# Attention scores in two 288-key halves, and the transposed q and k of a head pair side by side in one tile

## Chip, core and metric

One core of a Trainium2 chip runs the whole program. The metric is the time of one execution on the device, in microseconds (us); the time of a kernel is the median of its runs. The engines are TensorE (PE; its weight loads are shown as PEld), VectorE (DVE), ScalarE (ACT), GpSimd (POOL) and SyncE (SP). SP computes nothing here: it issues most of the transfers, in the order of its queue. Each engine works through its own queue in order.

## What is computed

Attention with a position bias, and two mixture-like feed-forward blocks behind it. The attention part is what the change touches.

```
B, H, S, D = 4, 8, 576, 64
scores = q @ k.T / sqrt(D) + bias[h]        # bias: a small network on log distances, per head
attn   = softmax(scores)
x      = attn @ v                            # 2304 tokens x 512
h      = max(x @ w1, x @ w2, x @ w3) @ w_out
out    = (sigmoid(h @ g) * (h @ u)) @ w_out2
```

## The kernel before

**Precision.** A float32 matrix is held as two float16 parts, high and low. Products are sums of float16 matmuls over such parts.

**Units and pairs.** There are 32 heads of 576 rows; a head has five row tiles (four of 128 rows, one of 64). Two heads make a pair P, and the ten units of a pair are its row tiles, the two heads in turn. The main loop runs over u, the 160 units. In iteration u it emits, among others: `emit_E` of unit u, `emit_X` (the exp), `emit_S` of unit u + 1, the later stages of units before, pieces of the first MoE (`moe1`, matmuls of 288 columns in `mm3`, line 797) as filling for TensorE, and at the end `prep(u)`. For the first eight heads (`by_pe`) TensorE transposes the attention weights itself (line 690) and GpSimd scales them (line 659); for the others SP transposes them by DMA (`emit_T`, line 702), and of every ten units some are worked on by GpSimd (lines 659 and 674).

**`prep`, the preparation of q and k.** It runs some 16 units ahead, by steps s of a pair (s = u + 16 - 10 P):
- steps 0 and 1: `load_qk`, q and k of both heads from HBM by SP (lines 359 and 360);
- steps 2 to 6: squares and scales;
- steps 6 and 7: `r_hi` for q, then for k, on GpSimd (line 402), steps 8 and 9: `r_lo` on VectorE (line 407). They write tile `R`, both heads at once;
- steps 10 and 11: `r_trans` (line 411), one DMA transpose on SP each, 1280 columns. Before, the one at step 10 is for the first head of the pair, q and k mixed, and that at step 11 for the second head;
- steps 14 and 15: `k_swap` for the first and the second head (lines 421 and 422): two VectorE copies that exchange the upper and lower 64 partitions of k (high and low part), into tile `k2`.

For pair 0 the transposes are at steps 8 and 9 and the swaps at 11 and 12, ahead of the main loop.

**`emit_S`** (lines 617 and 618) multiplies the q tile of a unit with k and then with k2, four matmuls: 512 columns into the first PSUM bank of a score tile and 64 into the second, twice. There are two score tiles. `put_sums` puts one-column matmuls (line 130) behind them into free columns of the same tile. **`emit_E`** (line 637) is one VectorE operation: scores plus bias, and the maximum of each row.

`v_shift` (lines 452 and 453) makes similar copies of v, at iterations 7 and 8 of ten, `v_hi` (line 440) its high part on GpSimd.

Of the kernel before, what the change touches and what calls it, by code (L numbers as in the profile page):

```python
# [11 lines left out]
F16 = mybir.dt.float16  # L12
# [3 lines left out]
ALU = mybir.AluOpType  # L16
# [48 lines left out]
def tile_kernel(ctx, tc, q, k, v, w1, b1, w2, mw1, mw2, mw3, mwo, gw, vw, ow, xtab, masks, out):  # L65
    nc = tc.nc
    B, H, S, D = q.shape
# [4 lines left out]
    NIT = 5  # L72
    rows = [128, 128, 128, 128, 64]
    HS = S // 2
# [34 lines left out]
    def end_tiny():  # L109
        tiny(len(tq))  # L110
# [13 lines left out]
    def put_sums(free, lag=False):  # L124

        c = 0
        now = sums[:ripe[0]] if lag else sums[:]
        for src, then in now:
            for i in range(src.shape[1]):
                nc.tensor.matmul(free[:, c:c + 1], lhsT=ones, rhs=src.bitcast(BF16)[:, 2 * i + 1:2 * i + 2],  # L130
                                 start=(i == 0), stop=(i == src.shape[1] - 1))
            summed.append((then, free[:, c:c + 1]))
            c += 1
        del sums[:len(now)]
        ripe[0] = len(sums)
# [25 lines left out]
    with tc.manual_schedule():  # L161
# [31 lines left out]
        def rpool(name, bufs):  # L193
            return at.enter_context(tc.tile_pool(name=name, bufs=bufs, side="right"))

        p1, p2, p3, p4 = rpool("p1", 1), rpool("p2", 2), rpool("p3", 3), rpool("p4", 4)
# [145 lines left out]
        kq_t, k2_t, v_t = {}, {}, {}  # L342
# [4 lines left out]
        R_t, qs_t, vs_t = {}, {}, {}  # L347
        rqk2 = slots[3][:, 0:1280].rearrange("p (j h t d) -> p j h t d", j=2, h=2, t=NIT)

        def rq(P):  # L350
            return rqk2 if P in (2, 4) else rqk
# [45 lines left out]
        def r_hi(P, j):  # L397

            if j == 0:
                R_t[P] = p1.tile([128, 2, NIT, 2, 2, D], F16, tag="R", name="R")  # L400
            s = qs_t[P][:, j:j + 1]
            nc.gpsimd.tensor_scalar(R_t[P][:, :, :, j, 0], rq(P)[:, j], s, 1.0, op0=ALU.mult, op1=ALU.mult)

        def r_lo(P, j):
            s = qs_t[P][:, j:j + 1]
            R = R_t[P]
            nc.vector.scalar_tensor_tensor(R[:, :, :, j, 1], rq(P)[:, j], s, R[:, :, :, j, 0], op0=ALU.mult, op1=ALU.subtract)

        def r_trans(n):
            kq = p4.tile([128, NIT, 2, 128], F16, tag="kq", name="kq")  # L410
            nc.sync.dma_start_transpose(
                out=kq.rearrange("p t j s -> p (t j) s"),
                in_=R_t[n // 2][:, n % 2].rearrange("p t j e d -> p (t j e d)"),
            )
            kq_t[n] = kq

        def k_swap(n):

            kq = kq_t[n]
            k2 = p4.tile([128, NIT, 128], F16, tag="k2", name="k2")  # L420
            nc.vector.tensor_copy(k2[0:64], kq[64:128, :, 1])
            nc.vector.tensor_copy(k2[64:128], kq[0:64, :, 1])  # L422
            k2_t[n] = k2

        def v_squares(b, j):
            if j == 0:
                vs_t[b] = p2.tile([128, PPB], F32, tag="vmx", name="vmx")
            squares(rvb[:, 2 * j:2 * j + 2].rearrange("p h t d -> p (h t d)"), vs_t[b][:, j:j + 1], False)

        def v_scales(b):  # L430
            vs_t[b], sc["uv", b] = up_down_sq(vs_t[b], f"v{b}")
# [23 lines left out]
        def prep(u):  # L455

            P, s = divmod(u, 10)
            b = P // PPB
            if 0 <= P < NP:
                j = P % PPB  # L460
                if P == 0 and s < 4:
                    v_squares(0, s)
                if j == 0:
                    if s == (2 if P else 3):
                        v_scales(b)
                    if s == (4 if P else 5):
                        end_tiny()
                if s in (5, 6):
                    v_hi(2 * P + s - 5)
                if s in (6, 7):  # L470
                    v_lo(2 * P + s - 6)
                if s in (7, 8) and not by_pe(2 * P + s - 7):
                    v_shift(2 * P + s - 7)

            if 0 <= P < NP - PPB and s == 8:
                load_v(b + 1, P % PPB)
            if P == -1 and 4 <= s < 8:
                load_v(0, s - 4)
            Pv = P - 1
            if 0 <= Pv < NP - PPB and s == (1 if Pv % PPB == PPB - 1 else 2):  # L480
                v_squares(Pv // PPB + 1, Pv % PPB)
            Pq, s = divmod(u + QLEAD + QEARLY, 10)
            if 2 <= Pq <= 5 and s < 2:
                load_qk(Pq, s)
            for Pq in range((u + QLEAD) // 10, (u + QLEAD) // 10 - 2, -1):
                s, n = u + QLEAD - 10 * Pq, 2 * Pq
                if not 0 <= Pq < NP:
                    continue
                lo, tr, sw = ((8, 10), 10, 14) if Pq else ((7, 8), 8, 11)
                if s in (0, 1) and not 2 <= Pq <= 5:  # L490
                    load_qk(Pq, s)
                elif s in (2, 3):
                    qk_squares(Pq, s - 2)
                elif s == 4:
                    qk_scales(Pq)
                elif s == 6:
                    end_tiny()
                if s in (6, 7):
                    r_hi(Pq, s - 6)
                if s in lo:  # L500
                    r_lo(Pq, lo.index(s))
                if s in (tr, tr + 1):
                    r_trans(n + s - tr)
                if s in (sw, sw + 1):
                    k_swap(n + s - sw)

# [4 lines left out]
        bias_t, e_t, ph_t, l_t, r_t, pt_t = {}, {}, {}, {}, {}, {}  # L511
# [97 lines left out]
        def emit_S(u):  # L609

            n, it = units[u]
            m = rows[it]
            kq, k2 = kq_t[n], k2_t[n]
            ps = ps_s.tile([128, 1024], F32, tag="s", name="s")
            qs = kq[:, it, 0, :m]
            for j, kk in enumerate((kq[:, :, 1], k2)):
                nc.tensor.matmul(ps[:m, 0:512], lhsT=qs, rhs=kk[:, 0:4], start=(j == 0), stop=(j == 1))  # L617
                nc.tensor.matmul(ps[:m, 512:576], lhsT=qs, rhs=kk[:, 4, 0:64], start=(j == 0), stop=(j == 1))
            put_sums(ps[:, 600:616])
            s_t[u] = ps  # L620

        ep_t, x_t, n_ep = {}, {}, [0]
# [6 lines left out]
        def emit_E(u):  # L629

            n, it = units[u]
            m = rows[it]
            ps = s_t.pop(u)
            e = new_ep(u)[:, 0:S] if by_pe(n) else p4.tile([128, S], F32, tag="e", name="e", bufs=NE)
            mx = p4.tile([128, 1], F32, tag="mx", name="mx")
            l = p4.tile([128, 1], F32, tag="l", name="l")
            nc.vector.tensor_tensor_reduce(e[:m], ps[:m, :S], bias_t.pop(u)[:m], -1.0, 3.0e38, ALU.add, ALU.min, mx[:m])  # L637
            e_t[u], l_t[u], x_t[u] = e, l, mx
            take_sums()

# [287 lines left out]
        for u in range(NU + 7):  # L928
            t = FEED[u // (10 * PPB)]
# [44 lines left out]
            for ua, g, late_, pe2 in ((3, 0, LA, False), (9, 1, LB, False), (3, 0, LA0, True), (9, 1, LB0, True)):  # L974
                w = u - ua - late_
                if w >= 0 and w % 10 == 0 and w // 10 < NP:
                    P = w // 10
# [296 lines left out]
```

## Time and profile before

| | us |
|---|---|
| median of three runs | 1083.96 |
| lowest and highest | 1082.88, 1093.58 |
| the profiled execution | 1085.36 |
| its span | 1083.5 |
| TensorE busy | 995.3 (92%) |
| VectorE busy | 689.5 (64%) |
| ScalarE busy | 549.1 (51%) |
| GpSimd busy | 189.1 (17%) |

The span is what the profiler saw of the execution; the little that lies around it belongs to the time. Matmuls are pipelined: the duration shown for one runs on while the next has started, so their cost is read from start to start. The busy shares are means over stages: a first one that makes the bias (to 97 us), attention with the first MoE mixed in (97 to 560 us), the rest of the first MoE, and from 645 us on the second MoE, which is matmuls throughout.

### The profile page before, as it was taken

How to read it: one execution, taken by the hardware profiler on the slowest of the kernel's cores; microseconds unless marked ns; L12 is line 12 of the kernel's file. 1: busy time of each engine (PE TensorE's matmuls, PEld its weight loads, DVE VectorE, ACT ScalarE, POOL GpSimd, SP SyncE). 2: the span in 40 equal slices, each digit the busy share in tenths (PEclk: the TensorE clock that was granted, in tenths of full speed). 3: DMA queues.
4: the chain of work that ended last, by engine and by line, in shares of the span. 5: the costliest groups of instructions: out<-in, count | busy, mean ns of one | idle time of the engine just before them, and what ended most of it. 6: DMA issues, size and time to landing. Idle time of an engine off the chain costs nothing.

```text
span 1083.5 us, 20167 instructions
## 1 busy us (share of the span) xinstructions
PE 995.3 (92%) x7620; PEld 659.7 (61%) x7620; DVE 689.5 (64%) x1764; ACT 549.1 (51%) x1089; POOL 189.1 (17%) x199
## 2 busy tenths in 40 slices
PE   6977889878898899889999999998999999999998
PEld 2223445556665567656777777776764666766743
DVE  7997768889986889878866867778521221322210
ACT  6997778666775767776654435534410111211100
POOL 1003544343432244223321100000000000000000
PEclk9998989989998999999999999999999999999999
DMA  7898878999999999989964332323001000000001
GB/s 226 298 262 236 192 194 224 248 230 183 222 249 198 185 222 242 243 176 213 212 135 128 108 96 79 111 85 97 1 10 38 12 10 11 10 11 10 11 20 39
DMA packets 242958, 148.53 MB, mean 137 GB/s; under 512 B 183085, under 2 KB 214061, under 8 KB 242861
## 3 DMA queue, kind: packets, MB, share of 16 engines
q1 hardware_dynamic: 221604, 104.77, 45.2%
q10 hardware_dynamic: 21256, 42.48, 14.6%
q8 instruction: 60, 0.98, 0.4%
q14 instruction: 38, 0.30, 0.1%
HBM read 89.53 MB, written 15.34 MB: 97 GB/s over the span
## 4 chain that ended last, share of the span: by engine, by line
PE 53%; DVE 21%; DMA 10%; ACT 7%; issue 5%; ACTq 1%; POOL 1%; SPq 1%; DVEq 0%; POOLq 0%
PE po L1212 13%; PE mm L797 12%; PE pg L797 8%; PE pvl L797 8%; DMA pt<-ph 5%; PE s L797 3%; PE s L617 3%; PE t L690 2%; PE mm L756 2%; PE mm L752 2%; DVE xT L543 2%; DMA bias<-bias_d 2%; DVE e L637 2%; ACT ph L662 1%; DVE gT L1187 1%
## 5 line engine op out<-in xcount | busy, mean ns | idle before, releaser
L797 PEld LDWEIGHTS <-slot 128*128 128x128 f16 x2304 | 221.4, 99 | 88.2 <-issue 25.3
L797 PE MATMUL mm<-xT,slot 128*128 128x288 f16 x1512 | 212.1, 294 | 14.4 <-ACT hm L818 10.4
L1212 PE MATMUL po<-OW,gT 128*128 128x512 f16 x648 | 141.3, 379 | 0.0
L797 PEld LDWEIGHTS <-GW 128*128 128x128 f16 x1152 | 112.8, 98 | 41.7 <-issue 8.9
L797 PEld LDWEIGHTS <-VW 128*128 128x128 f16 x1152 | 112.2, 98 | 28.3
L643 ACT ACTIVATE e<-e,mx 128x576 f32<-128x576 f32 (+1 forms) x120 | 92.5, 771 | 46.2 <-DVE mx L637 42.5
L797 PE MATMUL pg<-x,GW 128*128 128x288 f16 x864 | 113.4, 289 | 0.5 <-DVE x_e L154 0.5
L797 PE MATMUL pvl<-x,VW 128*128 128x288 f16 x864 | 111.7, 286 | 0.0
L1177 ACT ACTIVATE sg<-pg,ug 128x576 f32<-128x576 f32 x48 | 35.5, 739 | 145.0 <-PE pg L797 131.4
L1212 PEld LDWEIGHTS <-gT 128*128 128x128 f16 x648 | 63.4, 98 | 74.8
L1184 DVE SCALAR_TENSOR_TENSOR sg<-pvl,sg 128x576 f32<-128x576 f32 x48 | 36.2, 754 | 108.4 <-PE pvl L797 107.6
L677 DVE SCALAR_TENSOR_TENSOR ph<-e,r,ph 128x576 f16<-128x576 f32 (+1 forms) x92 | 83.1, 903 | 22.5 <-ACT ph L662 22.3
L637 DVE CUSTOM_DVE_ANT_0 e<-s,bias 128x576 f32<-128x576 f32 (+1 forms) x120 | 89.5, 746 | 7.9 <-DMA bias<-bias_d 5.1
L1186 ACT CAST gT<-sg 128x576 f16<-128x576 f32 x48 | 32.2, 672 | 107.1 <-DVE sg L1184 107.1
L662 ACT ACTIVATE ph<-e,r 128x576 f16<-128x576 f32 (+1 forms) x92 | 71.0, 772 | 22.0 <-DMA pt<-ph 11.2
L552 PE MATMUL bo<-xT,w2blk 128*32 128x512 f32 x192 | 60.3, 622 | 16.9 <-DVE xT L543 14.3
L617 PE MATMUL s<-k,kq 128*128 128x512 f16 (+1 forms) x160 | 63.1, 394 | 13.2 <-DVE k L422 13.2
L1217 DVE TENSOR_TENSOR ob<-po,uo 128x512 f32<-128x512 f32 x16 | 11.1, 692 | 96.8 <-PE po L1212 96.8
L617 PE MATMUL s<-kq 128*128 128x512 f16 (+1 forms) x160 | 63.9, 399 | 8.4 <-DVE mx L637 5.9
L797 PE MATMUL mm<-hT,slot 128*128 128x288 f16 x504 | 66.1, 286 | 0.0
L1187 DVE TENSOR_TENSOR gT<-sg,gT 128x576 f16<-128x576 f32 x48 | 36.4, 759 | 34.9 <-ACT gT L1186 34.9
L617 PEld LDWEIGHTS <-kq 128*128 128x128 f16 (+1 forms) x320 | 32.7, 102 | 39.5 <-issue 17.4
(203 smaller groups left out, 1652.0 us busy)
## 6 DMA issues: line engine op xcount, KB each, us to landing
bias<-bias_d ACTq DMA_DIRECT2D x128, 288.0 KB, 4.1
bias_d<-x SPq DMA_DIRECT2D x36, 288.0 KB, 4.3
x<-in_moe_w_dram SPq DMA_DIRECT2D x12, 768.0 KB, 6.5
w<-in_moe_w_gate_dram SPq DMA_DIRECT2D x12, 512.0 KB, 3.8
w<-in_moe_w_val_dram SPq DMA_DIRECT2D x12, 512.0 KB, 3.6
w<-in_moe_w_out_dram SPq DMA_DIRECT2D x12, 512.0 KB, 3.4
bias<-bias_d ACTq DMA_DIRECT2D x32, 144.0 KB, 4.7
out_dram<-ob SPq DMA_DIRECT2D x36, 128.0 KB, 2.3
```

The lines of the kernel that those rows point to most:

```text
L552: nc.tensor.matmul(bo[32 * g:32 * g + 32, 0:512], lhsT=lhsT, rhs=hs[4 * ti + g][:, :, 0:128], start=True, stop=True, tile_position=(0, 32 ...
L617: nc.tensor.matmul(ps[:m, 0:512], lhsT=qs, rhs=kk[:, 0:4], start=(j == 0), stop=(j == 1))
L637: nc.vector.tensor_tensor_reduce(e[:m], ps[:m, :S], bias_t.pop(u)[:m], -1.0, 3.0e38, ALU.add, ALU.min, mx[:m])
L643: nc.scalar.activation(e_t[u][:m], e_t[u][:m], AF.Exp, scale=-1.0, bias=x_t.pop(u)[:m], accum_out=l_t[u][:m])
L662: nc.scalar.activation(ph_t[u][:m, 0], e_t[u][:m], AF.Copy, scale=r[:m])
L677: nc.vector.scalar_tensor_tensor(ph[:m, 1], e_t.pop(u)[:m], r_t.pop(u)[:m], ph[:m, 0], op0=ALU.mult, op1=ALU.subtract)
L797: nc.tensor.matmul(ps[hf][:, :HS], lhsT=W(wp, kk), rhs=X(xp, kk)[:, hf * HS:(hf + 1) * HS], start=(first and i == 0), stop=(last and i == 2))
L1177: nc.scalar.activation(hm3(sg), pg[:, :, :HS], AF.Sigmoid, scale=ugm)
L1184: nc.vector.scalar_tensor_tensor(hm3(sg), pvl[:, :, :HS], DOWN2, hm3(sg), op0=ALU.mult, op1=ALU.mult)
L1186: nc.scalar.copy(gT[:, 0, m, c0:c0 + S], sg)
L1187: nc.vector.tensor_tensor(gT[:, 1, m, c0:c0 + S], sg, gT[:, 0, m, c0:c0 + S], op=ALU.subtract)
L1212: nc.tensor.matmul(po[:, 0, :], lhsT=gT[:, gi, kk, 128 * ct:128 * ct + 128], rhs=OW[:, wi, kk], start=(i == 0), stop=(i == 3 * K2 - 1))
```

## The change

- `R` is laid out with q of both heads first and k of both heads behind, and a transpose now takes q of both heads (step 10) or k of both heads (step 11). Both go into one tile per pair, with two such tiles in place of four tiles per head: the same memory.
- So each head's q tiles and k tiles lie side by side. The copies of `k_swap` read one run of 640 elements per partition where they read five runs of 128.
- The scores are four matmuls of 288 columns: two into the first bank, two into the second, and `emit_E` reads two runs of 288. `put_sums` takes columns 1000 to 1015 of the tile.

```
--- before.py
+++ after.py
@@ -397,29 +397,30 @@
         def r_hi(P, j):
 
             if j == 0:
-                R_t[P] = p1.tile([128, 2, NIT, 2, 2, D], F16, tag="R", name="R")
+                R_t[P] = p1.tile([128, 2, 2, NIT, 2, D], F16, tag="R", name="R")
             s = qs_t[P][:, j:j + 1]
-            nc.gpsimd.tensor_scalar(R_t[P][:, :, :, j, 0], rq(P)[:, j], s, 1.0, op0=ALU.mult, op1=ALU.mult)
+            nc.gpsimd.tensor_scalar(R_t[P][:, j, :, :, 0], rq(P)[:, j], s, 1.0, op0=ALU.mult, op1=ALU.mult)
 
         def r_lo(P, j):
             s = qs_t[P][:, j:j + 1]
             R = R_t[P]
-            nc.vector.scalar_tensor_tensor(R[:, :, :, j, 1], rq(P)[:, j], s, R[:, :, :, j, 0], op0=ALU.mult, op1=ALU.subtract)
-
-        def r_trans(n):
-            kq = p4.tile([128, NIT, 2, 128], F16, tag="kq", name="kq")
+            nc.vector.scalar_tensor_tensor(R[:, j, :, :, 1], rq(P)[:, j], s, R[:, j, :, :, 0], op0=ALU.mult, op1=ALU.subtract)
+
+        def r_trans(P, j):
+
+            if j == 0:
+                kq_t[P] = p4.tile([128, 2, 2, NIT, 128], F16, tag="kq", name="kq", bufs=2)
             nc.sync.dma_start_transpose(
-                out=kq.rearrange("p t j s -> p (t j) s"),
-                in_=R_t[n // 2][:, n % 2].rearrange("p t j e d -> p (t j e d)"),
+                out=kq_t[P][:, j].rearrange("p h t s -> p (h t) s"),
+                in_=R_t[P][:, j].rearrange("p h t e d -> p (h t e d)"),
             )
-            kq_t[n] = kq
 
         def k_swap(n):
 
-            kq = kq_t[n]
+            kk = kq_t[n // 2][:, 1, n % 2]
             k2 = p4.tile([128, NIT, 128], F16, tag="k2", name="k2")
-            nc.vector.tensor_copy(k2[0:64], kq[64:128, :, 1])
-            nc.vector.tensor_copy(k2[64:128], kq[0:64, :, 1])
+            nc.vector.tensor_copy(k2[0:64], kk[64:128])
+            nc.vector.tensor_copy(k2[64:128], kk[0:64])
             k2_t[n] = k2
 
         def v_squares(b, j):
@@ -500,7 +501,7 @@
                 if s in lo:
                     r_lo(Pq, lo.index(s))
                 if s in (tr, tr + 1):
-                    r_trans(n + s - tr)
+                    r_trans(Pq, s - tr)
                 if s in (sw, sw + 1):
                     k_swap(n + s - sw)
 
@@ -610,13 +611,14 @@
 
             n, it = units[u]
             m = rows[it]
-            kq, k2 = kq_t[n], k2_t[n]
+            kq, k2 = kq_t[n // 2], k2_t[n]
             ps = ps_s.tile([128, 1024], F32, tag="s", name="s")
-            qs = kq[:, it, 0, :m]
-            for j, kk in enumerate((kq[:, :, 1], k2)):
-                nc.tensor.matmul(ps[:m, 0:512], lhsT=qs, rhs=kk[:, 0:4], start=(j == 0), stop=(j == 1))
-                nc.tensor.matmul(ps[:m, 512:576], lhsT=qs, rhs=kk[:, 4, 0:64], start=(j == 0), stop=(j == 1))
-            put_sums(ps[:, 600:616])
+            qs = kq[:, 0, n % 2, it, :m]
+            for j, kk in enumerate((kq[:, 1, n % 2], k2)):
+                kk = kk.rearrange("p t s -> p (t s)")
+                for hf in range(2):
+                    nc.tensor.matmul(ps[:m, 512 * hf:512 * hf + HS], lhsT=qs, rhs=kk[:, HS * hf:HS * hf + HS], start=(j == 0), stop=(j == 1))
+            put_sums(ps[:, 1000:1016])
             s_t[u] = ps
 
         ep_t, x_t, n_ep = {}, {}, [0]
@@ -634,7 +636,8 @@
             e = new_ep(u)[:, 0:S] if by_pe(n) else p4.tile([128, S], F32, tag="e", name="e", bufs=NE)
             mx = p4.tile([128, 1], F32, tag="mx", name="mx")
             l = p4.tile([128, 1], F32, tag="l", name="l")
-            nc.vector.tensor_tensor_reduce(e[:m], ps[:m, :S], bias_t.pop(u)[:m], -1.0, 3.0e38, ALU.add, ALU.min, mx[:m])
+            halves = lambda t: t.rearrange("p (a s) -> p a s", a=2)
+            nc.vector.tensor_tensor_reduce(halves(e)[:m], halves(ps)[:m, :, :HS], halves(bias_t.pop(u))[:m], -1.0, 3.0e38, ALU.add, ALU.min, mx[:m])
             e_t[u], l_t[u], x_t[u] = e, l, mx
             take_sums()
```

## Rows read from the trace of the kernel before

**Rows 1.** Busy time in three stretches: PE, PEld, DVE, ACT, POOL, clock, DMA.
```profile
97.00:185.00 88.00, 75.95 (x504) 41.85 (x504) 66.12 (x233) 66.53 (x151) 45.43 (x62) 0.90 0.82 206
185.00:325.00 140.00, 121.21 (x996) 83.57 (x997) 122.91 (x334) 97.24 (x212) 54.53 (x50) 0.94 1.12 224
325.00:560.00 235.00, 213.95 (x1841) 151.08 (x1840) 196.50 (x558) 161.95 (x343) 72.49 (x71) 0.97 1.09 208
```
**Rows 2.** Timeline of TensorE, one unit: start us, duration us, engine, line, operation.
```profile
437.86 0.38 PE L617 MATMUL s<-kq 128*128 128x512 f16 x1
...
438.34 2.37 PE L797 MATMUL mm<-hT,slot 128*128 128x288 f16 x18
440.55 0.38 PE L617 MATMUL s<-kq 128*128 128x512 f16 x1
```
**Rows 3.** Waits of TensorE, 180 to 560 us: total, times, longest.
```profile
PE s L617 <- DVE k L422: 13.2, 10, 2.8
```
**Rows 4.** Groups of the page (busy, mean ns); single lines (ns min/median/max).
```profile
L1184 DVE SCALAR_TENSOR_TENSOR sg<-pvl,sg 128x576 f32<-128x576 f32 x48 | 36.2, 754 | 108.4 <-PE pvl L797 107.6
L637 DVE CUSTOM_DVE_ANT_0 e<-s,bias 128x576 f32<-128x576 f32 (+1 forms) x120 | 89.5, 746 | 7.9 <-DMA bias<-bias_d 5.1
...
L440 POOL TENSOR_SCALAR vh<-rvb,v_s x24: 526/806/1148, 193.6 to 548.4; 128x320 f16<-128x320 f32 x24
L402 POOL TENSOR_SCALAR R<-rqk,sqk x28: 791/798/2146, 34.4 to 509.6; 128x640 f16<-128x640 f32 x28
```
**Rows 5.** Copies on VectorE, single lines: ns min/median/max.
```profile
L421 DVE COPY k<-kq x32: 476/480/482, 68.9 to 530.9; 64x640 f16<-64x640 f16 x32
...
L452 DVE COPY vh<-vh x24: 251/252/1240, 198.7 to 555.7; 64x320 f16<-64x320 f16 x24
L453 DVE COPY vh<-vh x24: 221/222/223, 199.0 to 556.0; 64x256 f16<-64x256 f16 x24
```
**Rows 6.** Timeline of VectorE and GpSimd, at two copies.
```profile
310.68 0.48 DVE L421 COPY k<-kq 64x640 f16<-64x640 f16 x1
310.82 0.74 POOL L659 TENSOR_SCALAR e<-e,r 64x576 f32<-64x576 f32 x1 [3.92 <-ACT e L643]
...
430.62 1.28 POOL L674 TENSOR_TENSOR ph<-e,ph 128x576 f16<-128x576 f32 x1 [0.21 <-ACT ph L668]
430.77 1.24 DVE L452 COPY vh<-vh 64x320 f16<-64x320 f16 x1
```
**Rows 7.** Timeline: second transpose and first swap, first and last of eleven pairs.
```profile
198.45 1.57 SPq L411 DMA_TRANSPOSE kq<-R  x1
203.53 0.48 DVE L421 COPY k<-kq 64x640 f16<-64x640 f16 x1
...
518.92 2.08 SPq L411 DMA_TRANSPOSE kq<-R  x1
528.23 0.48 DVE L421 COPY k<-kq 64x640 f16<-64x640 f16 x1
```
**Rows 8.** Line 411, issue to landing: all 32; the transposes at 198.45 and 428.41.
```profile
DMA to landing us min/median/max: 4.1/6.2/8.3
...
DMA to landing us min/median/max: 5.8/5.8/5.8
...
DMA to landing us min/median/max: 8.0/8.0/8.0
```
**Rows 9.** TensorE at two first swaps, and the clock (third column from the right).
```profile
278.57 0.38 PE L617 MATMUL s<-k,kq 128*128 128x512 f16 x1 [2.83 <-DVE k L422]
435.36 0.38 PE L617 MATMUL s<-k,kq 128*128 128x512 f16 x1 [1.53 <-DVE k L422]
...
278.00:280.00 2.00, 1.43 (x11) 0.99 (x11) 1.96 (x6) 2.00 (x4) 0.00 (x0) 0.83 1.22 266
280.00:282.00 2.00, 2.00 (x10) 1.19 (x9) 1.92 (x5) 0.33 (x2) 0.74 (x1) 0.50 1.24 279
436.00:438.00 2.00, 2.00 (x18) 1.56 (x16) 1.92 (x8) 1.18 (x3) 0.00 (x0) 1.00 1.27 308
```

## The prediction

> **What bounds the kernel now.** I read the busy times by stretch first [rows 1]. Attention runs from 97 to 560 us. In its first stretch (heads whose attention TensorE transposes itself) TensorE is busy 86% of the time and VectorE 75%; in the next two TensorE is at 87% and 91%, VectorE at 88% and 84%. Both queues are in order and feed each other, so neither is "the" bound: what one loses at a hand-over the other usually loses too. After 560 us comes pure MoE, which the change doesn't touch. So it is worth only what it does to hand-overs within 460 us.
>
> The timeline of TensorE between two saturated stretches prices the scores [rows 2]: the four score matmuls of a unit start at 437.86, the MoE matmuls behind them at 438.34, and these, 18 of 288 columns, reach to 440.55. So the scores take 0.48 us and one 288-column matmul takes (440.55 - 438.34) / 18 = 0.123 us. The durations shown (0.38 for 512 columns) overlap and are not what a matmul costs.
>
> Then the waits of TensorE: it waited ten times, 13.2 us in all, for the second copy of `k_swap`, the longest 2.8 [rows 3]. That is the one hand-over in the stretch that the change touches directly.
>
> **Matmuls in halves.** Removed: two of 512 and two of 64 columns, 0.48 us. Added: four of 288, 4 x 0.123 = 0.49 us. Weight loads stay four. Nothing gained, nothing lost: 160 units x 0.01 us is at most 1.6 us and within the reading error of the two starts. The 64-column matmuls look like waste but are not.
>
> **VectorE reads the scores from two banks.** No row of before has this custom operation on such a pattern, but L1184 reads 2 x 288 out of two banks and takes 754 ns for 576 elements, where L637 takes 746 on a plain run [rows 4]. 8 ns x 160 = 1.3 us of VectorE at most; below, nothing. I take nothing, since the two rows are different operations.
>
> **`R` written in another order.** `r_hi` and `r_lo` write the same 640 elements; only the spacing of the 64-element runs halves. `v_hi` writes at the new spacing: 526 ns at the least for 320 elements; L402 at the old spacing 791 at the least for 640 [rows 4]. Half the elements cost two thirds, as with a fixed part, so the spacing shows no price: nothing. If it had one, at most 2 x 526 - 791 = 261 ns on POOL, 32 times, and POOL stands idle for most of the stretch.
>
> **The copies of `k_swap`.** Now the source is one run of 640; before it was five runs of 128 with gaps. L421 takes 480 ns, and never anything else (476 to 482); L452, also 16-bit and 64 partitions, takes 252 for 320 elements, L453 222 for 256 [rows 5]. The step between those two, 30 ns for 64 elements, carried on to 640 gives 222 + 6 x 30 = 402; and the cost can't be under 222. Bounds: 480 (copies as slow as now) and 222. L452 and L421 also differ in kind: L452 stretched to 1.24 us when POOL was in its L674 (four of 24 times), L421 kept to 0.48 with POOL's L659 starting 0.14 us into it [rows 6]. A contiguous copy should run in L452's manner, so between 222 and 402: I take the middle, 312, which saves 0.17 us per copy, 0.34 per swap.
>
> The Trainium skill's page VectorE: DVE Perf Modes (The perf-mode tier table; Side-by-side) says that 16-bit copies within SBUF run four elements per cycle beside some 158 fixed cycles; for 640 elements that would be an estimate of 331 ns, and a saving of 0.30 per swap in place of 0.34.
>
> First swap of a pair (at step 14): TensorE waited for it in ten of the eleven pairs from 185 us on, so 10 x 0.34 = 3.4 us less on the path. Second swap (step 15): no wait behind it; seven of eleven run free of POOL, 7 x 0.34 = 2.4 us of VectorE. In the other four, and in all eight swaps before 185 us, POOL's L659 starts inside the first copy. If POOL now takes its turn between the two copies, the second waits for it: about 0.14 + 0.2 + 0.74 + 0.1 = 1.2 against 0.98 now, some 0.2 more, 12 x 0.2 = 2.4 us. These two cancel.
>
> **What waits for the transposes.** This is the part that speaks against the change. The two transposes of a pair keep their places (steps 10 and 11), but the second now holds the k of both heads. Before, the first swap at step 14 needed only the first transpose, four steps earlier; now it needs the second, three steps earlier. On the SP queue nothing is moved: the second transpose goes out behind the same pt transpose and the same two loads. (The first no longer waits for the second `r_lo`; that helps before 185 us, where both are issued back to back, and not later, where the loads ahead of it were out after `r_lo` anyway.) So the landing of the second transpose in before can be set against the start of the first swap. From issue to first copy, over eleven pairs from 198.45/203.53 to 518.92/528.23 [rows 7]: 5.1, 7.6, 6.1, 4.9, 4.6, 4.6, 5.2, 5.9, 7.1, 4.4, 9.3 us. From issue to landing: 4.1 to 8.3, median 6.2; shown for five of the eleven: 5.8, 4.8, 6.2, 5.2, 8.0 (pairs 1, 2, 4, 6, 8) [rows 8]. With the median for the rest the swap would wait 0.7, 0, 0.1, 1.3, 1.6, 0.6, 1.0, 2.1, 0, 1.8, 0. The first pair has 2.6 us of slack at TensorE; the rest add up to 8.4. Bounds: unknown landings at 4.1 give 3.9 in all, at 8.3 (or at the second swap's start, by which they had landed) some 16.
>
> While the swap waits, VectorE's queue stands: behind it L637 of the next unit, whose maximum ScalarE's exp needs and whose score buffer TensorE needs. TensorE stands already, since its first score matmul of the pair reads the same k. Both engines shift together, so I count the wait in full.
>
> **Sum of the likeliest case**: +8.4 (landing) - 3.4 (first swaps) + 2.4 - 2.4 (second swaps, collisions) = +5.0 us. The profiled execution took 1085.4, 1.4 above the median of the runs; on the median, 1084.0 + 5 = 1089.
>
> **Rivals.**
> *Landing hidden.* VectorE lags a little more everywhere, or transposes land near 4 to 5 us, and only shorter copies remain: -3.4 to -5.8, so 1078 to 1081. For it: four of the distances are 6 us or more. Against: the landing at 428 us was shown at 8.0.
>
> *The clock falls.* Where TensorE stood 2.83 us for the swap, the granted clock went to 0.83 and then to 0.50 (1.2 of 2.4 GHz) over the next 4 us; where it stood 1.53 us it stayed at 1.00 [rows 9]. The lost clock is 0.17 x 2 + 0.5 x 2 = 1.3 us at least per fall. Five pairs get a landing wait of 1 us or more on top of waits that average 1.3; if all five then stand long enough, +5 + 5 x 1.4 = +12: 1096. It decides where the waits for k grow from the size that kept the clock (1.53) towards the one that was followed by the fall (2.83). Against: the wait is cut in two now (first for the landing, then for the copies, with two matmuls between).
>
> *Cancelled by POOL.* L452's rows [rows 6] show a copy held for the whole rest of a POOL instruction. If each of the 12 swaps that meet POOL loses 0.74 - 0.34 = 0.4 us, that is +4.8, and with the landing hidden -5.8 + 4.8 = -1: 1083, a change that does nothing. The Trainium skill's SBUF — State Buffer (Who interferes with whom) states the rule: a copy in a two-port mode and a GpSimd instruction exclude each other fully; by that rule, the trace agrees with 1.24 against 0.25 us.
>
> **How the numbers follow.** Landing wait as summed: 0.50, 1085 to 1094. Landing hidden: 0.22, about 1080. Clock falls: 0.18, 1095 to 1101. Cancelled: 0.10, about 1083. Range: from 1078 (hidden) to 1098 (clock, half of it), which leaves out some 0.15; the likeliest case alone has 1085 to 1094. Faster by over 1% (under 1073.1) needs a gain that I find no row for: 0.03. Slower by over 1% (over 1094.8): the clock case and the edge of the first, 0.20. Within 1%, about what runs of this kernel can tell from no change: 0.77.
>
> **What would show it.** Right: L421 and L422 at 0.3 us or a little over; a new wait of VectorE at L421 for the transposes, some 8 us in five to eight places; TensorE's wait for k grown from 13 to about 18 us, part of it now for the DMA; L659 of POOL late, or L422 long, in 12 places; score matmuls of 288 columns at 0.12 us start to start. Wrong: copies still at 0.48; no wait for the transposes; TensorE time per unit other than 0.49; or a clock that falls at the first unit of a pair where it did not before. The forecast would be wrong above all if the landings of the six unknown pairs were all early.

## The result, and the profile after

The changed kernel took 1088.18 us in the median of 14 runs (1080.29 to 1099.12), the kernel before 1084.99 in as many runs beside it (1075.03 to 1093.58). The ratio of after to before is 1.0059, with a 95% interval of 1.0033 to 1.0086: slower by some 6 us, under one per cent. The medians differ by half of that, 3.2 us. (Ratios here and below leave out executions more than 1.5% above the fastest of their kernel, medians count all.) The forecast was 1089, or +0.46%, by a longer wait for the transposes less the gain of shorter copies.

The two profiled executions can't be set against each other as wholes: the one of after happened to take 1085.27 us, 3 us under its own median, and both spans are 1083.5. So the profile is read term by term here, and the sizes of effects come from the ratios.

One thing that stands above the prediction has to be put right first. The list of steps gives `r_lo` at steps 8 and 9; the code (line 490, quoted in the second experiment) has 8 and 10, so k's low part is made right ahead of the first transpose. No term of the sum uses it, but it is why k can't be transposed before step 10.

**Copies.** In the kernel after, the two copies of `k_swap` are lines 422 and 423 (single lines: ns min/median/max, first and last start):

```profile
L422 DVE COPY k<-kq x32: 316/322/324, 68.7 to 530.6; 64x640 f16<-64x640 f16 x32
...
L423 DVE COPY k<-kq x32: 319/321/781, 69.0 to 531.0; 64x640 f16<-64x640 f16 x32
```

A copy out of one run takes 0.32 us where one out of five runs took 0.48 [rows 5], and the first of the two is never held up. The second takes up to 0.78. The timelines of VectorE and GpSimd after, at one such place:

```profile
274.94 0.32 DVE L422 COPY k<-kq 64x640 f16<-64x640 f16 x1
275.28 0.78 DVE L423 COPY k<-kq 64x640 f16<-64x640 f16 x1
...
275.08 0.80 POOL L662 TENSOR_SCALAR e<-e,r 64x576 f32<-64x576 f32 x1 [5.84 <-ACT e L646]
```

GpSimd's line 662 (659 before, [rows 6]) starts 0.14 us into the first copy, and the second copy ends 0.18 us after it. This happens in 12 of the 32 swaps: in all eight between 97 and 185 us and in the second swaps of the four pairs behind them.

**Waits.** VectorE and TensorE after, 180 to 560 us (waiting engine, tile and line, what ended the wait: total us, times, longest), and the landings of all 32 transposes:

```profile
DVE k L422 <- DMA kq<-R: 6.3, 5, 2.3
...
PE s L620 <- DMA kq<-R: 7.7, 4, 2.4
PE s L620 <- DVE k L423: 6.1, 10, 1.6
...
DMA to landing us min/median/max: 4.4/6.7/9.0
```

VectorE now stands at the first swap until the second transpose has landed; there was no such wait before. TensorE's one wait for the swapped k [rows 3] is cut in two, first for the landing, then for the copies, 13.8 us together against 13.2. The landings (4.1/6.2/8.3 in [rows 8]) came half a microsecond later in this execution.

**Matmuls and the two-bank read.** TensorE after, one unit between two saturated stretches, as in [rows 2], and the page's group for the custom operation, as in [rows 4]:

```profile
437.54 0.41 PE L620 MATMUL s<-kq 128*128 128x288 f16 x2
437.79 0.41 PE L620 MATMUL s<-k,kq 128*128 128x288 f16 x2
438.03 2.37 PE L800 MATMUL mm<-hT,slot 128*128 128x288 f16 x18
440.24 0.41 PE L620 MATMUL s<-kq 128*128 128x288 f16 x2
...
L640 DVE CUSTOM_DVE_ANT_0 e<-s,bias 128x576 f32<-128x576 f32 (+1 forms) x120 | 89.6, 747 | 8.3 <-DMA bias<-bias_d 3.5
```

The scores take 438.03 - 437.54 = 0.49 us, 0.48 before; one 288-column matmul takes (440.24 - 438.03) / 18 = 0.123 us, as before. Reading two banks costs 747 ns against 746. (The weight loads are busy 247.2 us between 180 and 560 us with halves and 237.3 before the change, 2848 and 2870 of them; start to start the matmuls show nothing of it.)

**Clock.** Busy times of after around the longest landing wait and around the fourth longest of the five (PE, PEld, DVE, ACT, POOL; the third column from the right is TensorE's granted clock), and TensorE's first scores at the same places:

```profile
303.00:305.00 2.00, 0.03 (x1) 0.06 (x2) 0.14 (x1) 1.55 (x5) 0.00 (x0) 1.00 1.24 163
305.00:307.00 2.00, 1.81 (x10) 1.07 (x11) 1.96 (x6) 0.66 (x1) 0.00 (x0) 0.62 1.19 323
307.00:309.00 2.00, 2.00 (x10) 1.29 (x9) 1.92 (x5) 0.88 (x4) 0.80 (x1) 0.53 1.13 292
...
402.00:404.00 2.00, 2.00 (x19) 1.60 (x17) 1.92 (x8) 1.65 (x3) 0.00 (x0) 1.00 1.28 223
...
304.97 0.41 PE L620 MATMUL s<-kq 128*128 128x288 f16 x2 [2.40 <-DMA kq<-R]
...
400.87 0.41 PE L620 MATMUL s<-kq 128*128 128x288 f16 x2 [1.47 <-DMA kq<-R]
```

Where TensorE stood 2.40 us for the landing, the granted clock was 0.62 and 0.53 in the next 4 us, half of full speed or 1.2 GHz for most of it; where it stood 1.47 us it stayed at 1.00. It also fell behind the waits of 2.05 and 1.77 us, at 370 and 500 us. In the kernel before, none of these three pairs had a fall; others had, as at 278 us [rows 9]. Over 180 to 560 us in steps of 2 us, the granted clock falls seven times before and eight times after, and (1 - clock) x 2 us adds up to 15.4 in both. The windows of [rows 1] say the same, 0.94 and 0.97 before, and after:

```profile
185.00:325.00 140.00, 120.15 (x1003) 86.57 (x1003) 123.68 (x334) 96.40 (x208) 54.39 (x49) 0.95 1.08 224
325.00:560.00 235.00, 214.80 (x1820) 158.29 (x1815) 193.05 (x553) 161.81 (x338) 72.35 (x69) 0.96 1.09 205
```

### The profile page after: what moved, and what is told of

It is laid out like the page before. It is cut to its first block, busy times and chain, and to the rows that moved or that the text cites. A ratio compares the mean times of both kernels' runs of the same rounds, so it can differ in the third digit from the quotient of the medians.

```text
span 1083.5 us, 20182 instructions
## 1 busy us (share of the span) xinstructions
PE 996.1 (92%) x7620; PEld 675.8 (62%) x7620; DVE 691.7 (64%) x1764; ACT 551.6 (51%) x1089; POOL 189.0 (17%) x199
## 4 chain that ended last, share of the span: by engine, by line
PE 51%; DVE 25%; DMA 10%; ACT 6%; issue 5%; SPq 1%; ACTq 0%; POOL 0%; DVEq 0%; POOLq 0%
PE po L1215 13%; PE mm L800 12%; PE pg L800 8%; PE pvl L800 8%; PE s L800 3%; DMA pt<-ph 3%; PE s L620 3%; PE mm L759 2%; DMA kq<-R 2%; DMA bias<-bias_d 2%; DVE e L640 2%; DVE xT L544 2%; DVE ph L680 1%; DVE gT L1190 1%; DVE wf L93 1%
## 5 line engine op out<-in xcount | busy, mean ns | idle before, releaser
L800 PEld LDWEIGHTS <-slot 128*128 128x128 f16 x2304 | 226.3, 100 | 90.6 <-issue 30.2
L646 ACT ACTIVATE e<-e,mx 128x576 f32<-128x576 f32 (+1 forms) x120 | 92.9, 774 | 55.2 <-DVE mx L640 51.2
L620 PEld LDWEIGHTS <-kq 128*128 128x128 f16 (+1 forms) x640 | 59.6, 102 | 59.0 <-issue 44.1
L680 DVE SCALAR_TENSOR_TENSOR ph<-e,r,ph 128x576 f16<-128x576 f32 (+1 forms) x92 | 81.9, 891 | 19.6 <-ACT ph L665 18.1
L620 PE MATMUL s<-kq 128*128 128x288 f16 (+1 forms) x320 | 68.6, 297 | 16.8 <-DMA kq<-R 7.7
L553 PE MATMUL bo<-xT,w2blk 128*32 128x512 f32 x192 | 63.0, 638 | 15.4 <-DVE xT L544 13.3
L620 PE MATMUL s<-k,kq 128*128 128x288 f16 (+1 forms) x320 | 67.9, 295 | 7.6 <-DVE k L423 7.4
```

Of the source, the lines that this page charges most:

```text
L553: nc.tensor.matmul(bo[32 * g:32 * g + 32, 0:512], lhsT=lhsT, rhs=hs[4 * ti + g][:, :, 0:128], start=True, stop=True, tile_position=(0, 32 ...
L620: nc.tensor.matmul(ps[:m, 512 * hf:512 * hf + HS], lhsT=qs, rhs=kk[:, HS * hf:HS * hf + HS], start=(j == 0), stop=(j == 1))
L646: nc.scalar.activation(e_t[u][:m], e_t[u][:m], AF.Exp, scale=-1.0, bias=x_t.pop(u)[:m], accum_out=l_t[u][:m])
L680: nc.vector.scalar_tensor_tensor(ph[:m, 1], e_t.pop(u)[:m], r_t.pop(u)[:m], ph[:m, 0], op0=ALU.mult, op1=ALU.subtract)
L800: nc.tensor.matmul(ps[hf][:, :HS], lhsT=W(wp, kk), rhs=X(xp, kk)[:, hf * HS:(hf + 1) * HS], start=(first and i == 0), stop=(last and i == 2))
```

## The experiments

The theory: the change loses by the landing of k's transpose, which is now the second of the pair, and wins a little by shorter copies; the halves do nothing. Rivals: the collisions with GpSimd cost what is lost; the halves (288 columns, two-bank read) cost it; the clock does. Every ratio below is to the kernel before, run beside it on the same chip in the same session, with its 95% interval. There were three sessions, the first (k first, a step earlier, 512 + 64, a step later) on another chip than the other two; before had medians of 1083.87, 1082.74 and 1084.02 us in them.

All waits in one table, from the views of waits of each profiled execution, 180 to 560 us, total us (times). The last column is ScalarE's exp waiting for the maximum that VectorE makes; it shows how long VectorE's queue stood.

| kernel | ratio | VectorE, swap for transpose | TensorE for transpose | TensorE for swapped k | ScalarE for maximum |
|---|---|---|---|---|---|
| before | 1 | none | none | 13.2 (10) | 42.5 (35) |
| after | 1.0059 | 6.3 (5) | 7.7 (4) | 6.1 (10) | 51.2 (44) |
| after, again | 1.0040 | 7.4 (5) | 10.4 (5) | 6.0 (9) | 47.3 (41) |
| after, 512 + 64 | 1.0117 | 4.6 (3) | 7.8 (4) | 7.3 (10) | 48.3 (44) |
| the same, again | 1.0028 | 9.4 (6) | 9.2 (6) | 5.8 (9) | 51.3 (42) |
| before, heads exchanged | 1.0045 | 6.4 (3) | 8.6 (5) | 11.3 (11) | 52.9 (42) |
| after, a step later | 1.0118 | 21.8 (8) | 19.6 (8) | 3.9 (10) | 72.3 (47) |
| k first | 0.9982 | not read | not read | not read | not read |
| k first, again | 1.0026 | none | 10.9 (7) | 5.0 (5) | 40.9 (37) |
| k first, 512 + 64 | 1.0006 | none | 8.5 (5) | 7.7 (8) | 42.6 (36) |
| k first, swaps ahead | 0.9987 | none | 4.1 (4) | 3.8 (4) | 36.0 (35) |
| after, a step earlier | 1.0067 | none | none | 15.2 (10) | 44.2 (36) |
| four transposes | 1.0044 | none | none | 11.7 (9) | 39.5 (35) |
| before, copies twice | 1.0184 | none | none | 25.9 (15) | 69.4 (42) |

### k transposed first

```diff
-            if j == 0:
+            if j == 1:
...
-                    r_trans(Pq, s - tr)
+                    r_trans(Pq, 1 - (s - tr))
```

Everything else of the change is kept: layouts, copies, halves. k of both heads now goes out at step 10 and q at step 11.

> The changed kernel with the two transposes of a pair exchanged: k of both heads at step 10, q of both heads at step 11. Landing theory (the first swap waits for the second transpose): VectorE's 6.3 us of waiting for the transposes at line 422 go to 0, since k is now issued one step earlier. TensorE's wait at the first unit of a pair moves to the landing of q, and the copies no longer come behind that landing, so about 0.65 us less in each of the five pairs that waited, plus VectorE's work not shifted: 3 to 5 us less than the changed kernel, a ratio to the kernel before of 0.999 to 1.003. Rival (the loss comes from the copies that meet GpSimd, or from the 288-column scores): the order of the transposes is worth nothing, 1.004 to 1.008.

Measured: 0.9982 (0.9940 to 1.0025), median 1083.62. Its waits are read from the repeat below. In this run the loss is gone with the order, a little further than I had expected (0.999 to 1.003), and neither halves nor collisions account for that, since both are kept. The repeat lies higher.

### The same order, one step earlier

```diff
-                lo, tr, sw = ((8, 10), 10, 14) if Pq else ((7, 8), 8, 11)
+                lo, tr, sw = ((8, 10), 9, 14) if Pq else ((7, 8), 7, 11)
```

q at step 9, k at step 10.

> The changed kernel with both transposes one step earlier: q at step 9, k at step 10. q needs only the r_lo of step 8 for that, which the new layout allows. Landing theory: neither VectorE at line 422 nor TensorE at the first unit of a pair waits for these transposes any more (6.3 and 7.7 us in the changed kernel go to 0 or nearly), the shorter copies remain as a gain: 5 to 8 us less than the changed kernel, ratio to the kernel before 0.995 to 1.000. Rival (copies that meet GpSimd, or the 288-column scores, are the loss): no difference from the changed kernel, 1.004 to 1.008.

Measured: 1.0067 (1.0038 to 1.0096), median 1091.35: a miss. The landing wait did go, and the time stayed lost. ScalarE and VectorE in this kernel, 180 to 560 us:

```profile
ACT junk_w L371 <- DMA rqk<-in_q_dram: 23.3, 9, 4.0
...
DVE ph L680 <- ACT ph L665: 28.6, 27, 4.7
...
DVE r L651 <- ACT e L646: 9.6, 8, 2.3
```

The first was 14.4 us in the kernel after, the second 17.2, the third 4.2; in the kernel before they were 16.0, 21.4 and 3.6. SP's queue shows why, first in after, then in this kernel, at the same pair:

```profile
258.11 0.68 SPq L359 DMA_DIRECT2D rqk<-in_q_dram  x1
258.83 0.62 SPq L360 DMA_DIRECT2D rqk<-in_q_dram  x1
259.50 1.58 SPq L413 DMA_TRANSPOSE kq<-R  x1
...
260.93 2.09 SPq L413 DMA_TRANSPOSE kq<-R  x1
263.06 0.66 SPq L359 DMA_DIRECT2D rqk<-in_q_dram  x1
263.77 0.61 SPq L360 DMA_DIRECT2D rqk<-in_q_dram  x1
```

A step earlier, the transpose goes out ahead of the next pair's load of q instead of behind it. ScalarE then waits longer for that load, before its squares (line 371), and VectorE waits 38.2 us for ScalarE in the last two lines, 21.4 in after and 25.0 before. My expectation priced what the step gains at the swap and not what it moves back on SP. That the new waits are the whole of the loss fits, but no run tests it. So this run doesn't bear out the landing theory, which had forecast a gain here, and doesn't refute it either, since the step changed more than the landing.

### 512 + 64 columns in the kernel after

```diff
-                kk = kk.rearrange("p t s -> p (t s)")
-                for hf in range(2):
-                    nc.tensor.matmul(ps[:m, 512 * hf:512 * hf + HS], lhsT=qs, rhs=kk[:, HS * hf:HS * hf + HS], start=(j == 0), stop=(j == 1))
+                nc.tensor.matmul(ps[:m, 0:512], lhsT=qs, rhs=kk[:, 0:4], start=(j == 0), stop=(j == 1))
+                nc.tensor.matmul(ps[:m, 512:576], lhsT=qs, rhs=kk[:, 4, 0:64], start=(j == 0), stop=(j == 1))
```

with the plain reading of the custom operation behind it, and `put_sums` back in columns 600 to 615.

> The changed kernel with the scores as before, 512 and 64 columns, one run of 576 for VectorE; layout, transposes and copies stay changed. Landing theory: the halves cost and give nothing (0.48 against 0.49 us a unit), so this is the changed kernel again, 1.003 to 1.009 of the kernel before, with the waits for the transposes at line 422 as large. Rival (the halves are the loss, by the read from two banks or by their weight loads): 0.998 to 1.002.

Measured: 1.0117 (1.0087 to 1.0147), median 1093.73, above what either expected. Taken alone it would say that the halves are worth half a per cent. I ran it once more, in another session and on another chip:

> The changed kernel with scores of 512 and 64 columns, once more: it came out at 1.0117 where the changed kernel had 1.0059 and 1.0040, though the score matmuls of a unit take the same 0.48 to 0.50 us. If the halves are worth something, again 1.009 to 1.014; if that was of the session, 1.003 to 1.008.

Measured: 1.0028 (0.9993 to 1.0063), median 1089.23. The two intervals of one kernel don't meet, so ratios differ between sessions (or chips) by more than their intervals say, here by 0.9%. That is more than the whole effect of the change, and it bears on every single ratio here. The mean of the two, 1.007, lies beside that of after, 1.005. The same exchange was made with k first:

> The kernel with k transposed first (0.998), and the scores back in 512 and 64 columns. The kernel with 512 and 64 columns alone had come out 0.6% above the changed kernel, against the forecast. If the halves are worth that much by themselves, this one is 1.002 to 1.006; if that difference was of the session or of the interplay of queues in that one kernel, it is 0.995 to 1.001, and the score matmuls of a unit take 0.48 to 0.50 us in both.

Measured: 1.0006 (0.9972 to 1.0040), median 1085.11; the two runs with k first and halves have 1.0004 in the mean. Halves or not, no difference shows beyond what sessions differ by, and start to start the scores take the same time.

### One step later

```diff
-                lo, tr, sw = ((8, 10), 10, 14) if Pq else ((7, 8), 8, 11)
+                lo, tr, sw = ((8, 10), 11, 14) if Pq else ((7, 8), 9, 11)
```

> The changed kernel with both transposes one step later (q at 11, k at 12), so that the first swap comes two units behind the transpose of k in place of three. Landing theory: a unit is 2.9 us, so each of the eleven pairs from 185 us on waits up to that much longer, less the slack of the six that did not wait: 15 to 32 us more than the changed kernel, 1.02 to 1.035 of the kernel before, with VectorE's wait for the transposes at 25 us or more. If the clock falls at each of these longer waits, another 10 us. Rival: the distance is of no account, 1.004 to 1.008.

Measured: 1.0118 (1.0067 to 1.0169), median 1097.13, less than I expected. VectorE and TensorE in this kernel, 180 to 560 us:

```profile
DVE k L422 <- DMA kq<-R: 21.8, 8, 4.2
...
PE s L620 <- DMA kq<-R: 19.6, 8, 3.5
```

The wait at VectorE grew by 15.5 us over the kernel after, the time by 1.0118 against 1.0059 and 1.0040, which is 6 to 8.5 us. So about half of a wait there reached the end, if that; I had counted it in full. (Against the 1.0117 of the same session it would be none of it, by the medians of those two kernels 3.4 us. Neither the share nor, by this run alone, the sign is sure.)

### The kernel after, again, and the landing alone in the kernel before

> The changed kernel once more, unchanged, to see how far a ratio of one session repeats in another and to have its number on the same chip as the three kernels beside it. All theories: 1.003 to 1.009 of the kernel before.

Measured: 1.0040 (1.0001 to 1.0078), median 1089.42, beside 1.0059.

The other run leaves the kernel before as it is but for the order of its two transposes. There the second head's tile, not needed until step 15, goes out first, and the first head's, needed at step 14, second:

```diff
-                    r_trans(n + s - tr)
+                    r_trans(n + 1 - (s - tr))
```

> The kernel before with nothing changed but the order of its two transposes: the second head of a pair at step 10, the first head at step 11. So the first swap waits for the transpose of three steps ago, as in the changed kernel, while layout, copies (0.48 us) and scores stay as before. Landing theory: VectorE waits some 5 to 9 us for the transposes at line 421, in five to eight places. In the kernel with both transposes a step later 15.5 us more of this wait cost 6.5 us of time, so 2 to 8 us here: 1.002 to 1.007. Rival (the loss of the changed kernel comes from the copies that meet GpSimd, or from the tile layout): 0.998 to 1.001.

Measured: 1.0045 (1.0008 to 1.0081), median 1088.13. Its waits, 180 to 560 us:

```profile
DVE k L421 <- DMA kq<-R: 6.4, 3, 3.9
...
PE s L617 <- DMA kq<-R: 8.6, 5, 4.6
PE s L617 <- DVE k L422: 11.3, 11, 1.9
```

Old layout, old copies, old matmuls, and still the waits of the kernel after (6.4 against 6.3 and 7.4 us at VectorE) and its loss. A landing one step later is enough to make it. The wait at VectorE came in three places, not in the five to eight that I expected, and one of them has 3.9 of the 6.4 us. Layout, copies and halves are ruled out as a need for the loss by this run, as far as one session can do it: the interval begins at 1.0008.

### Four transposes instead of two

```diff
-            nc.sync.dma_start_transpose(
-                out=kq_t[P][:, j].rearrange("p h t s -> p (h t) s"),
-                in_=R_t[P][:, j].rearrange("p h t e d -> p (h t e d)"),
-            )
+            for j in range(2):
+                nc.sync.dma_start_transpose(
+                    out=kq_t[P][:, j, h],
+                    in_=R_t[P][:, j, h].rearrange("p t e d -> p (t e d)"),
+                )
```

q and k of the first head at step 10, of the second at step 11: the new layout with the old order of arrival.

> The changed kernel with four transposes of 640 columns in place of two of 1280: q and k of the first head at step 10, of the second head at step 11. Layout, copies and scores stay changed, but the first swap needs only transposes of step 10, as before the change. Landing theory: VectorE's wait at line 422 goes to about 0, and 5 to 9 us of the changed kernel come back: 0.995 to 1.001, unless four transposes hold the SP queue much longer than two, which their durations would show. Rival (copies, layout): 1.004 to 1.008, as the changed kernel.

Measured: 1.0044 (1.0013 to 1.0076), median 1086.26: a miss. The transposes of this kernel as a single line (ns min/median/max), and what ScalarE waited for:

```profile
L414 SPq DMA_TRANSPOSE kq<-R x64: 1200/1288/2358, 54.2 to 522.4; - x64
...
ACT junk_w L371 <- DMA kq<-R: 28.0, 8, 6.0
```

VectorE no longer waits at the swap. But a transpose of 640 columns holds SP 1.29 us in the median, some 70% of one of 1280 (1.81 in after), so two of them take 2.6 us per step. Of the waits before ScalarE's squares, 28.0 us are now put down to the transposes and 4.3 to the load of k; in after they were 14.4 and 5.8, for the loads of q and of k, and before the change 16.0 and 7.9. VectorE's waits for ScalarE, as read one step earlier, come to 33.9 us. So here too a wait at ScalarE's squares stands where the one at the swap was. By which way is not shown: SP issues the loads ahead of the transposes of the same step, so the order of its queue doesn't explain why the squares wait for the transposes.

### k first, again

> The changed kernel with k transposed first, once more, beside the kernel that moves the swaps ahead, and for a profile of it: 0.996 to 1.000 of the kernel before, no wait of VectorE for the transposes at line 422, TensorE's waits at the first unit of a pair for the transposes and the copies together 8 to 13 us (13.8 in the changed kernel).

Measured: 1.0026 (0.9993 to 1.0058), median 1088.14. That is above the range that I expected, and no lower than the 1.0028 which q first with 512 + 64 columns has in the same session. Its waits, 180 to 560 us:

```profile
PE s L620 <- DMA kq<-R: 10.9, 7, 2.6
...
PE s L620 <- DVE k L423: 5.0, 5, 1.5
```

Now q lands last, and TensorE waits for it, 15.9 us in both lines, more than I expected and no less than in after. The difference is that VectorE doesn't stand: the swap needs k alone, and the row of VectorE's wait for the transposes is gone. ScalarE waits for the maximum 40.9 us, as before the change (42.5), against 51.2 and 47.3.

### Swaps ahead of the reciprocal

With k first, `k_swap` is called just ahead of `emit_hi` instead of within `prep`, so that the copies are done before the reciprocal that GpSimd's line 659 (662) waits for.

```diff
-                if s in (sw, sw + 1):
-                    k_swap(n + s - sw)
...
+            swaps(u)
             for x in at_step(u, 1):
                 emit_hi(x)
```

> The kernel with k transposed first, and each swap moved ahead within its iteration: in front of the reciprocal that releases GpSimd's L659, and of the copies of v, in place of behind them. Collision theory (GpSimd's turn between the two copies costs time in 12 swaps): the second copy takes 0.32 us everywhere and no longer 0.78 in 12 places, and k is ready about 0.15 to 0.6 us sooner at the ten first swaps that TensorE waits for, so 2 to 6 us less than with k first alone: 0.993 to 0.998 of the kernel before. Rival (the collisions are hidden, and what is moved ahead of the reciprocal only delays the weights of attention): 0.998 to 1.002.

Measured: 0.9987 (0.9938 to 1.0035). The collisions are gone, as this line of the kernel shows:

```profile
L423 DVE COPY k<-kq x32: 320/321/323, 69.4 to 521.7; 64x640 f16<-64x640 f16 x32
```

and no gain over k first is clear of the noise: the two ratios of k first are 1.0026, beside it, and 0.9982 in the first session. The twelve runs reach from 1075.2 to 1095.8 us, and their median, 1088.5, is 0.4% above that of before where the ratio says 0.1% below. So what the collisions cost is not shown; k first has them too and comes out at 1.0004 in the mean, so they don't make the loss of the changed kernel by themselves.

### The price of VectorE's time at this place

The kernel before with every swap's two copies made twice, 0.98 us more per swap, 32 x 0.98 = 31 us:

```diff
+            for _ in range(2):
...
```

> The kernel before with the two copies of each swap made twice (0.98 us more of VectorE per swap, 31 us in all), to see how much of a copy's time reaches the end. By the accounting of the forecast the first swaps of ten pairs count in full, 9.8 us, and the second swaps in part: 1.009 to 1.014 of the kernel before. If a swap is mostly hidden, 1.000 to 1.005, and the shorter copies of the changed kernel (0.34 us a swap) can't have given back more than a third of that.

Measured: 1.0184 (1.0133 to 1.0235), median 1105.16, more than I expected. 0.0184 x 1084 = 20 us for 31 us of VectorE: 0.64 of it reached the end. VectorE's time at the swap is worth something after all, though VectorE is busy only 64% of the span.

## Why the prediction held, step by step

**The total** (1089, +0.46%) and its direction came out: 1.0059 and 1.0040, 1088.18 and 1089.42 us. The wait that it was built on is in the profiles. Its terms were less exact than its sum, though: the landing was counted in full and came to less in time, and the gain of the copies, set against it, isn't seen in any run. That two errors of opposite sign left the sum where it was is in part luck.

**The landing wait** is the cause that the runs support, by three comparisons. After and its repeat against k first and its repeat: 1.005 against 1.0004. All four with q first (512 + 64 columns among them) against all four with k first: 1.006 against 1.000. And the kernel before with only the landing moved: 1.0045. The sign agrees in all three, the size is less sure: by the medians of all executions the four with q first are at 1.0058 of before and the four with k first at 1.0025, half the difference, and in the last session it nearly vanishes (1.0028 against 1.0026 and 0.9987). Single profiles don't separate the two orders: `emit_E` of the 24 heads from 180 us on takes, from its first start to its last, 373.4 to 378.7 us in the four with q first, 376.9 and 373.7 in two with k first, 374.1 before (381.3 with the heads exchanged). And the two other kernels without the wait at the swap lost as much (1.0067 and 1.0044), which I put down to new waits for ScalarE without a run that tests it.

I had forecast 8.4 us at VectorE in five to eight places; the profiles have 6.3 and 7.4 in five. The method (second transpose's issue plus its landing, against the first swap's start, pair by pair, [rows 7, 8]) found the size but only some of the places: for pairs 4 to 10, by first swap, I had 1.3, 1.6, 0.6, 1.0, 2.1, 0 and 1.8 us, and it was 2.35, 0, 0.22, 0.68, 0, 1.05 and 2.02. The landing of pair 8, which the trace of before showed at 8.0 us and which I took as the surest, was no wait at all.

**Counted in full** was too much as a rule: of the wait added by a step later about half at most reached the end. Where the loss of the landing alone (0.0045 x 1083 = 4.9 us) stands against its 6.4 us at VectorE, it is three quarters (0.9 to 8.8 us by the interval). And "both engines shift together" was not quite the mechanism. With k first TensorE waits as long (15.9 us) and less is lost, if anything; what differs is VectorE standing, which ScalarE's wait for the maximum follows in the table.

**The copies**: 312 ns taken, 320 to 322 measured, between the 480 and 222 of the bounds. The estimate of 331 by the Trainium skill's VectorE: DVE Perf Modes (The perf-mode tier table; Side-by-side) was as near. Twenty clean swaps save 0.33 us each; the twelve with GpSimd take 0.33 + 0.78 = 1.11 us where 0.98 had been, and I had said about 1.2. At the measured 0.64, (20 x 0.33 - 12 x 0.13) x 0.64 = 3 us should come back. With k first, where the landing wait of VectorE is gone, that would be 0.997; measured are 0.9982, 1.0026 and, with 512 + 64 columns, 1.0006. The gain of the copies is thus not shown by any run, nor excluded. From 4.9 for the landing and 3 for the copies the change should cost some 2 us, while 4 to 6 are measured. **What makes up the difference stays open**: TensorE's new wait for q, the collisions, and the spread between sessions are all of its size.

**TensorE's wait for k**: 13.8 and 16.4 us in the two profiles of after, 18 forecast, and part of it for the DMA, as said.

**Collisions**: the 12 swaps that I named are the 12 that collide, in the order that I gave (first copy free, GpSimd's instruction, second copy held). This agrees with the rule that I cited from the Trainium skill's SBUF — State Buffer (Who interferes with whom): the held copy takes 0.78 us, the free one 0.32. They don't make the loss by themselves, as k first shows; the run with swaps ahead is too wide to price them.

**Halves, two banks, `R`'s order**: nothing, as taken: 0.49 us a unit, 747 ns, and 800 ns for `r_hi` against 798. The 64-column matmul that looks wasteful costs 0.02 to 0.03 us from its start to the next at the full clock in the profiles that have it.

**The clock** is where I was half wrong. I gave the case 0.18 and put its price on top. The mechanism did occur, at three of the five pairs with a landing wait, the very sign that I had named as speaking against my forecast. But falls that before had elsewhere were absent, and the sum of lost clock is the same 15.4 us. In the other profiles it is 11.9, 15.4 and 20.5 with q first (after, again; 512 + 64; the same, again), 12.0, 12.0 and 13.6 with k first (again; 512 + 64; swaps ahead), 18.8 with the heads exchanged in before and 22.2 a step later. In the mean q first thus has 3.3 us more of it than k first, but profiles of one kernel differ by as much, so what share of the loss goes by way of the clock is open too.

**Hidden** and **cancelled** didn't happen: the wait was there in five pairs, and the time was not that of before.

## What to carry to other kernels

When a transfer is regrouped so that one consumer needs less of it and another more, look for the consumer that comes first, and issue first what it needs: the same bytes in the other order are worth some 0.3 to 0.6% here, in the mean of four kernels each way. Before moving an issue to an earlier place, list what it passes on its queue, since in two of two attempts a wait removed at the swap was followed by longer ones around ScalarE and a time no better than after's. And where the effect is half a per cent, repeat the kernel in another session before an interval is believed: the same kernel gave 1.0117 and then 1.0028.

## What the runs showed of the hardware

- Where a GpSimd instruction started during the first of two copies that VectorE has back to back, it ended before the second in 12 of 12 places; the second copy then takes 0.78 us instead of 0.32, while the GpSimd instruction itself shows 0.77 to 0.80 us, against 0.74 beside the slower copies of the kernel before [rows 6].
- A copy's duration depends on the runs of its source: 640 elements from one run take 0.32 us, from five runs 0.48, with the same bytes and partitions.
- A DMA transpose of 640 columns occupies the issuing queue 1.20 to 2.36 us (median 1.29), one of 1280 columns 1.30 to 3.51 (median 1.81) in after: four small ones instead of two large ones cost the queue 1.5 us more per pair.
